# Linear attention with a feed-forward layer: maxima over partitions by GpSimd from batch 2 on, and subtractions in even steps

## The chip, the cores and the metric

The kernel runs on one core of a Trainium2 chip. The metric is the device time of one execution in microseconds (us), lower being better. Engines: PE is TensorE, DVE is VectorE, ACT is ScalarE, POOL is GpSimd, SP is SyncE.

## The reference

Two operators follow each other. The attention has 8 batches of 8 heads, 576 tokens and 64 dimensions, in float32; the feed-forward layer takes its 4608 tokens of 512 values through 2048 hidden values.

```python
q_s = softmax(q, over the head dimension)       # exp(q - max), divided by its sum
k_s = softmax(k, over the 576 tokens)           # exp(k - max), divided by its sum
kv  = einsum('bhsd,bhse->bhde', k_s, v)
x   = einsum('bhsd,bhde->bhse', q_s, kv)        # -> (4608, 512)
h   = x @ w_in                                  # 512 -> 2048
g   = h * erf(softplus(h))
out = g @ w_out                                 # 2048 -> 512
```

The tokens of a batch lie on the partitions, so k's maximum over tokens is one over partitions: 512 maxima (8 heads of 64), each over 576 tokens.

## The kernel before

The feed-forward layer is cut into 48 items. Item n is 384 tokens (`bk`, three blocks to a pair of batches) by 512 hidden values (`g`). Its first product `mm1` is a scheme with seven half-size products in four steps, m n.0 to m n.3. Each product goes into one of three PSUM banks, pX, pY and pZ, of which there is a single copy, and a VectorE add or copy or a ScalarE copy reads it into H: pY by a VectorE copy (line 1010), pX by an add (1012, "X0's add"), pZ and pX by ScalarE copies (1015, 1017), pX by an add (1020, "X2's add"), pZ by an add (1023, "Z's add"), pX by a ScalarE copy (1025). The next product into the same bank waits for its reader. In the text X0, X1, X2, X3 are the four products into pX of one item, in order. Then come T (softplus) and G (erf) on ScalarE, U (`gmul`, line 1078, g = G times H) on VectorE, a cast of g to float16 (1092), `glo` (1096, what the cast left) on VectorE, and, two items later, the second product `mm2` into banks o_0, o_1 and o_2 (line 1124), written out by line 1140 (ob). Items 0 to 5 use float32 products (1037, 1115).

The attention of batches 1 to 7 is one Python generator, `attention(b)`, stepped between the items' parts. Each `yield` gives a share of work (`SHARES`), and a pacer steps the generator until the sum of shares has reached a goal that grows with the item. For items 0 to 5 a string, `ORDER`, says by hand when steps ("A") come; `Z` in it is `wscales`, the scales of the weights from their row sums, with eight transposes through PE. What a step issues goes to in-order engine queues. Where it stands among the other instructions of an engine is set when the program is built, by a scheduler that takes the issued order as priority, unless `tc.issue_after` holds it behind a given instruction.

In a batch: `k_max` takes the maxima over a partition's tokens into `asc[:, 0]` (lines 518, 519, 522). `k_max_T` transposes them on PE (kT, line 529, four pieces) and reduces them on VectorE to km (533). `k_max_rows` spreads km over all partitions by four more transposes (kB, 544). Then k (two halves) and the tail kt are reduced by kB (704, 709), q by its own maxima (`q_sub`, lines 465 and 466, a reduction and a subtraction for each half, and for the pair's tail qt in odd batches), and five or six exponentials follow on ScalarE (349). kv's products are line 565. `all_max` (125, 127) does the same for one column: the scale of x is found from mx, the largest value of kv in a partition, by a transpose into x_bk and a reduction. Lines 301 and 393 split x into a float16 and a rest.

Of the kernel before, what the change touches and what calls it, by code (L numbers as in the profile page):

```python
# [1 line left out]

# [11 lines left out]
ALU = mybir.AluOpType  # L14
AX = mybir.AxisListType
PSUM = bass.MemoryType.PSUM


JOBS = [
# [16 lines left out]
    m0.0 m0.1 D0.0.1 D0.1.1 D1.0 D1.1 m0.2 m0.3 T0 G0 Q0  # L36
    D2.0 A m1.0 D2.1 m1.1 U0 m1.2 m1.3 T1 G1 Q1 A A D3.0 M0.0 D3.1 M0.1 M0.2 Q2 U1 A A
    m2.0 D4.0 m2.1 D4.1 m2.2 m2.3 T2 G2 Q3 A A D5.0 M1.0 D5.1 M1.1 M1.2 U2 A A Q4 D6.0
    m3.0 D6.1 m3.1 D7.0 m3.2 D7.1 m3.3 T3 G3 A A A A A A A A A A Q5 U3 Q6 Q7
    M2.0 M2.1 M2.2 m4.0 m4.1 Z m4.2 m4.3 T4 G4 M3.0 f0 M3.1 M3.2 S0 R0 m5.0 m5.1 U4 m5.2 m5.3  # L40
    T5 G5 f1 S1 R1
"""

# [13 lines left out]
def attn_moe_kernel(  # L57
# [9 lines left out]
    nc = tc.nc  # L67
# [51 lines left out]
    WIN = 7 * 512  # L119


    def all_max(mx, name):

        bk = psa.tile([P, 512], F32, tag="bk", name=f"{name}_bk")
        nc.tensor.transpose(bk[:, :P], mx.to_broadcast([P, P]), ident)
        e = at.tile([P, 1], F32, tag="sc_e", name=f"{name}_e")
        nc.vector.tensor_reduce(e, bk[:, :P], axis=AX.X, op=ALU.max)
        nc.vector.tensor_scalar_max(e, e, TINY)
        return e

    def scale_of_max(mx, name):

        e = all_max(mx, name)
        nc.vector.tensor_scalar(
            e.bitcast(I32), e.bitcast(I32), EXPMASK, None, op0=ALU.bitwise_and
        )
        s = at.tile([P, 1], F32, tag="sx", bufs=3, name=f"{name}_s")
        u = at.tile([P, 1], F32, tag="ux", bufs=3, name=f"{name}_u")
        nc.vector.reciprocal(s, e)
# [330 lines left out]
    def q_norm(t, g, name, b, o=None):  # L470
# [12 lines left out]
        for f in range(2):  # L483
# [86 lines left out]

    E32, QDMA = 2, 3
    kv32 = [t.rearrange("p h c e -> p (h c e)").bitcast(F32) for t in kvh]
    kv32 = [t.rearrange("p (c e) -> p c e", c=NC4) for t in kv32]

# [23 lines left out]
    def kv_split(b, mx):  # L600

        d = bat[b]
        s, u = scale_of_max(mx, f"x{b}")
        d["sx"], d["ux"] = s, u
        if b >= E32:
            hi, lo = (kvh[b % 2][:, i] for i in range(2))
            nc.vector.tensor_scalar_mul(hi, d["kvf"], s)
            nc.vector.scalar_tensor_tensor(
                lo, d["kvf"], s, hi, op0=ALU.mult, op1=ALU.subtract
            )  # L610
        d["U"] = at.tile([P, NG], F32, tag="U", bufs=3, name=f"U_{b}")
        if b > 1:
            nc.vector.tensor_scalar_mul(d["U"], w_u["in"], d["ux"])
# [78 lines left out]
    def attention(b):  # L692
        d, j, p = bat[b], b % 2, b // 2
        even = bat[b - j]
        tl = slice(j * TAIL, (j + 1) * TAIL)
        ks, qs, kt = d["k"], d["q"], even["kt"][tl]
        kmax = k_max(b, ks, (kt, tl))
        yield SHARES[0]
        km = k_max_T(b, kmax)
        q_sub(rows(qs[0]), 16, f"q_{b}_0")  # L700
        yield SHARES[1]
        kb = k_max_rows(b, km)
        for hf in range(2):
            nc.vector.tensor_tensor(
                ks[hf], ks[hf],
                kb[:, None, hf * 4:hf * 4 + 4, :].to_broadcast([P, TM, 4, D]),
                op=ALU.subtract,
            )
        nc.vector.tensor_tensor(kt, kt, kb[tl], op=ALU.subtract)
        yield SHARES[2]  # L710
        q_sub(rows(qs[1]), 16, f"q_{b}_1")
        if j == 1:
            q_sub(even["qt"], H, f"qt_{p}")
        yield SHARES[3]
        for t in (*ks, kt, qs[0], qs[1], *([even["qt"]] if j == 1 else [])):
            act(t, t, AF.Exp, chain=b > 1)
        yield SHARES[4]
        kv_norm(b, 0, kv_mm(b, 0))
        if b > 1:
            d["v"].append(load_half(v, "v", b, 1))  # L720
        q_norm(rows(qs[0]), 16, f"q_{b}_0", b)
        yield SHARES[5]
        if b >= QDMA:
            q_turn_half(b, 0)
        kv_norm(b, 1, kv_mm(b, 1))
        if b + 1 < B:
# [12 lines left out]
        yield SHARES[8]
        for i in ((3 * p + 1, 3 * p + 2) if j else (3 * p, 3 * p + 1)):  # L740
            while not x_free(i):
                yield 0

        def tails():
            if b < QDMA:
                bk = bank(f"qTt_{p}")
                for c in range(NC4):
                    nc.tensor.transpose(
                        bk[:, c * P:(c + 1) * P], asc[:, 1, c * P:(c + 1) * P], ident
                    )  # L750
                even["qtT"] = q_evac(b, 0, bk)
            yield SHARES[9]
            qT = even["qtT"]
            bks = [bank(f"xt_{p}_{a}") for a in range(2)]
            x = xblock(p * NBK + 1)
            for j_ in range(2):
                for hf in range(2):
                    oc = slice(hf * P + j_ * TAIL, hf * P + (j_ + 1) * TAIL)
                    qs_ = [
                        qT[:, :, (2 * hf + c) * P + j_ * TAIL:(2 * hf + c) * P + (j_ + 1) * TAIL]  # L760
                        for c in range(2)
                    ]
# [12 lines left out]
            yield SHARES[10]  # L775

        if j == 1 and b < QDMA:
            yield from tails()
        for hf in range(2):
            if hf == 1 and j == 1 and b >= QDMA:  # L780
                yield from tails()
            qTs = []
            for c in (2 * hf, 2 * hf + 1):
                qTs.append(q_T(b, c, bank(f"qT_{b}_{c}")) if b < QDMA else d["qT"][c])
                if b < QDMA and c % 2 == 1 and b + 1 < B:
                    load_q(b + 1, hf)
# [187 lines left out]
    def mm1(n, k):  # L974
# [29 lines left out]
        def bank2(b):  # L1004
            return s[b][:, :T].rearrange("p (a t) -> p a t", a=2)

        add = nc.vector.tensor_tensor
        if k == 0:
            prod("Y", 1, 1)
            nc.vector.tensor_copy(C[0, 0], bank2("Y"))  # L1010
            prod("X", 0, 0)
            add(C[0, 0], bank2("X"), C[0, 0], op=ALU.add)  # L1012
        elif k == 1:
# [58 lines left out]
    def gmul(n):  # L1072
        s, g = st[n], seq[n][2]
        if n < NG:
            nc.vector.tensor_tensor(flat(s["G"]), flat(s["G"]), flat(s["H"]), op=ALU.mult)
            return
        assert "all" in wready
        nc.vector.scalar_tensor_tensor(  # L1078
            flat(s["G"]), flat(s["G"]), GA32 if n < N32 else GA[:, g:g + 1], flat(s["H"]),
            op0=ALU.mult, op1=ALU.mult,  # L1080
        )
# [11 lines left out]

    def glo(n):
        s = st[n]
        nc.vector.tensor_tensor(flat(s["gl"]), flat(s["G"]), flat(s["gh"]), op=ALU.subtract)  # L1096

    acc = {}

# [177 lines left out]
```

## Time and profile before

| | us |
|---|---|
| median of 3 runs (lowest to highest) | 837.88 (837.61 to 839.1) |
| the profiled execution | 839.42 |
| its span, first to last instruction | 837.6 |
| PE busy | 811.6 (97%) |
| VectorE busy | 624.0 (74%) |
| ScalarE busy | 503.9 (60%) |
| GpSimd busy | 15.9 (2%) |

The profiled execution is one execution, 1.54 us above the median; 1.8 us of it lie outside its span. Busy time of an engine says how long it worked, not whether something waited for it. In the groups of instructions the last column is the engine's idle time just before that group, with what ended it. In the timelines each row has its start, its duration, engine, line, operation, the tiles written and read and the number of merged instructions; brackets hold idle time ahead of it.

### The profile page before, as it was taken

Reading aid. Unit: us, or ns where it says so; the run is one execution under the profiler, and the core shown is the slowest. Engines: PE = TensorE matmul, PEld = TensorE weight load, DVE = VectorE, ACT = ScalarE, POOL = GpSimd, SP = SyncE. Lnnn points to the kernel's source line nnn. Section 1 sums busy time; section 2 is a strip of 40 time slices with the busy share of each in tenths; the row PEclk is TensorE's granted clock in tenths of the full one; section 3 lists DMA queues with packets and bytes.
Section 4 is the critical chain, followed back from the end, with each engine's and each line's share of the span. In section 5 each row is a group of like instructions: output and inputs, shape, how many; then the busy total and the mean of one; then the engine's idle time right before and its main releaser. Section 6 shows DMA issues by size and latency. Waiting matters only on the chain.

```text
span 837.6 us, 15532 instructions
## 1 busy us (share of the span) xinstructions
PE 811.6 (97%) x6546; PEld 547.3 (65%) x6546; DVE 624.0 (74%) x887; ACT 503.9 (60%) x645; POOL 15.9 (2%) x37
## 2 busy tenths in 40 slices
PE   5999999999999999999999999999999999999996
PEld 4555455676666667767676676766776766767762
DVE  6999889998898779767875779857875657554543
ACT  2797759876665746645754556555764565544432
POOL 2101000000000000000000000000000000000000
PEclk9999999999999999999999999999999999999999
DMA  9995710041127205311362204411130100100100
GB/s 259 408 223 183 185 44 38 1 108 39 51 55 154 77 1 105 91 27 27 84 125 51 64 2 93 104 26 27 54 62 14 39 1 1 39 1 1 39 1 38
DMA packets 141348, 61.55 MB, mean 73 GB/s; under 512 B 130528, under 2 KB 132576, under 8 KB 141280
## 3 DMA queue, kind: packets, MB, share of 16 engines
q1 hardware_dynamic: 139104, 52.18, 25.1%
q0 software_dynamic: 2176, 8.39, 2.8%
q8 instruction: 51, 0.84, 0.4%
q14 instruction: 17, 0.14, 0.1%
HBM read 45.09 MB, written 9.44 MB: 65 GB/s over the span
## 4 chain that ended last, share of the span: by engine, by line
PE 59%; DVE 19%; ACT 13%; DMA 4%; issue 3%; SPq 2%; ACTq 0%; DVEq 0%
PE o L1124 25%; PE pX L998 14%; PE pZ L998 6%; ACT G L349 4%; ACT L349 4%; PE pY L998 3%; DVE G L1078 3%; DVE H L1096 2%; PE o L1115 2%; SPq L420 2%; DMA q<-in_q_dram 2%; PE pX L1037 2%; PE kv L565 1%; DVE x L301 1%; PE x L680 1%
## 5 line engine op out<-in xcount | busy, mean ns | idle before, releaser
L1124 PE MATMUL o<-wt,H 128*128 128x512 f16 x1512 | 347.3, 379 | 1.7 <-DVE H L1092 1.3
L998 PEld LDWEIGHTS <-wt 128*128 128x128 f16 x3528 | 293.1, 98 | 37.3 <-issue 15.8
L1124 PEld LDWEIGHTS <-H 128*128 128x128 f16 x1512 | 145.9, 98 | 150.9 <-DVE H L1092 1.8
L998 PE MATMUL pX<-x,wt 128*128 128x192 f16 x2016 | 194.3, 246 | 6.2 <-DVE H L1020 3.3
L349 ACT ACT_TABLE_LOAD x104 | 133.4, 1283 | 8.7 <-DVE H L1023 6.9
L1078 DVE SCALAR_TENSOR_TENSOR G<-G,small,H 128x1536 f32<-128x1536 f32 x44 | 80.0, 1818 | 55.3 <-ACT G L349 55.2
L1025 ACT COPY H<-pX 128x384 f32<-128x384 f32 x42 | 19.9, 474 | 139.2 <-PE pX L998 139.2
L998 PE MATMUL pZ<-x,wt 128*128 128x192 f16 x1008 | 98.4, 246 | 0.0
L349 ACT ACTIVATE G<-H,U 128x768 f32<-128x768 f32 (+1 forms) x56 | 69.2, 1253 | 22.1 <-DVE H L1023 21.5
L1096 DVE TENSOR_TENSOR H<-G,H 128x1536 f16<-128x1536 f32 x42 | 73.7, 1755 | 0.8
L349 ACT ACTIVATE G<-G 128x1536 f32<-128x1536 f32 x48 | 71.2, 1484 | 0.5
L998 PE MATMUL pY<-x,wt 128*128 128x192 f16 x504 | 48.4, 246 | 0.0
L454 ACT ACTIVATE x<-x 128x384 f32<-128x384 f32 (+1 forms) x52 | 16.2, 397 | 48.0 <-PE x L680 48.0
L1023 DVE TENSOR_TENSOR H<-pZ,H 128x384 f32<-128x384 f32 x42 | 23.2, 552 | 26.3 <-PE pZ L998 26.2
L1010 DVE COPY H<-pY 128x384 f32<-128x384 f32 x42 | 23.2, 553 | 26.1 <-PE pY L998 26.0
L300 ACT ACTIVATE x<-x 128x768 f16<-128x768 f32 (+1 forms) x44 | 33.0, 764 | 15.4 <-DVE x L393 15.4
L1092 DVE CAST H<-G 128x1536 f16<-128x1536 f32 x42 | 40.2, 957 | 0.8
L301 DVE SCALAR_TENSOR_TENSOR x<-x,x 128x768 f16<-128x768 f32 (+1 forms) x44 | 37.3, 851 | 3.2 <-ACT x L300 3.2
L1140 DVE TENSOR_SCALAR ob<-o,V 128x512 f32<-128x512 f32 x29 | 21.7, 747 | 21.1 <-PE o L1124 21.1
L1037 PE MATMUL pX<-x,wt 128*128 128x384 f32 x96 | 34.0, 488 | 0.0
L1012 DVE TENSOR_TENSOR H<-pX,H 128x384 f32<-128x384 f32 x42 | 23.3, 555 | 13.7 <-PE pX L998 12.9
L465 DVE TENSOR_REDUCE q_m<-q 128x16 f32<-128x1024 f32 x14 | 17.0, 1216 | 18.0 <-DMA q<-in_q_dram 18.0
(183 smaller groups left out, 818.8 us busy)
## 6 DMA issues: line engine op xcount, KB each, us to landing
out_dram<-ob SPq DMA_DIRECT2D x32, 256.0 KB, 2.3
vbuf<-in_v_dram SPq DMA_DIRECT2D x56, 128.0 KB, 3.2
q<-in_q_dram SPq DMA_DIRECT2D x56, 128.0 KB, 3.2
k<-in_k_dram SPq DMA_DIRECT2D x56, 128.0 KB, 3.2
wt<-in_moe_w_out_dram POOLq DMA_DIRECT2D x5, 1024.0 KB, 6.5
wt<-in_moe_w_in_dram SPq DMA_DIRECT2D x4, 1024.0 KB, 12.0
wt<-in_moe_w_out_dram SPq DMA_DIRECT2D x2, 1024.0 KB, 15.7
H_raw<-in_k_dram SPq DMA_DIRECT2D x2, 512.0 KB, 4.6
```

The costliest lines, as they stand in the source:

```text
L300: nc.scalar.activation(hi, src, AF.Copy, scale=s)
L301: nc.vector.scalar_tensor_tensor(lo, src, s, hi, op0=ALU.mult, op1=ALU.subtract)
L349: i = nc.scalar.activation(out_, in_, func, **kw)
L998: nc.tensor.matmul(o, w[wl][:, c, a * P:(a + 1) * P], x[:, xl, xi, c, :], start=(new and a == 0 and c == 0 and i == 0), stop=(c == 1 and i ...
L1010: nc.vector.tensor_copy(C[0, 0], bank2("Y"))
L1012: add(C[0, 0], bank2("X"), C[0, 0], op=ALU.add)
L1023: add(C[0, 1], bank2("Z"), C[0, 1], op=ALU.add)
L1037: nc.tensor.matmul(ph[:, :T], w[:, c, a * P:(a + 1) * P], x[:, c, :], start=(c == 0), stop=(c == NC4 - 1),)
L1078: nc.vector.scalar_tensor_tensor(flat(s["G"]), flat(s["G"]), GA32 if n < N32 else GA[:, g:g + 1], flat(s["H"]), op0=ALU.mult, op1=ALU.mult,)
L1092: nc.vector.tensor_copy(flat(s["gh"]), flat(s["G"]))
L1096: nc.vector.tensor_tensor(flat(s["gl"]), flat(s["G"]), flat(s["gh"]), op=ALU.subtract)
L1124: nc.tensor.matmul(o, s[gt][:, a, ts_], w[wl][:, a, :], start=(first_ and a == 0 and i == 0), stop=(last_ and a == FG - 1 and i == 2),)
```

## The change

From batch 2 on (`KPOOL = 2`), k's maximum over partitions and the maximum for x's scale are computed by `nc.gpsimd.partition_all_reduce`, which reads and writes SBUF and leaves the result on all partitions. The PE transposes and the VectorE reduction between them are not issued for those batches. k and kt are then reduced by `asc[:, 1]` in SBUF and not by kB in PSUM.

For those batches, the first four yields (2.51, 0, 0.16 and 0.09) become four of 0.69 each: maxima and the GpSimd reduction; both halves of k; kt and q's first half; q's second half and, in odd batches, qt. Each is held behind the last VectorE instruction issued so far by an item's Y copy, adds, gmul or glo (`own` records it, `behind` holds). In `ORDER` eight A's stand where ten did, and Z comes ahead of m4.0 instead of behind m4.1.

```diff
-    m3.0 D6.1 m3.1 D7.0 m3.2 D7.1 m3.3 T3 G3 A A A A A A A A A A Q5 U3 Q6 Q7
-    M2.0 M2.1 M2.2 m4.0 m4.1 Z m4.2 m4.3 T4 G4 M3.0 f0 M3.1 M3.2 S0 R0 m5.0 m5.1 U4 m5.2 m5.3
+    m3.0 D6.1 m3.1 D7.0 m3.2 D7.1 m3.3 T3 G3 A A A A A A A A Q5 U3 Q6 Q7
+    M2.0 M2.1 M2.2 Z m4.0 m4.1 m4.2 m4.3 T4 G4 M3.0 f0 M3.1 M3.2 S0 R0 m5.0 m5.1 U4 m5.2 m5.3
...
-    def all_max(mx, name):
-        bk = psa.tile([P, 512], F32, tag="bk", name=f"{name}_bk")
-        nc.tensor.transpose(bk[:, :P], mx.to_broadcast([P, P]), ident)
+    def all_max(mx, name, pool):
         e = at.tile([P, 1], F32, tag="sc_e", name=f"{name}_e")
-        nc.vector.tensor_reduce(e, bk[:, :P], axis=AX.X, op=ALU.max)
+        if pool:
+            nc.gpsimd.partition_all_reduce(e, mx, P, RED.max)
+        else:
+            ...
...
+    def own(ins):
+        dve[0] = ins.ins
+        return ins
+
+    def behind():
+        return tc.issue_after(dve[0]) if dve[0] else ExitStack()
...
-    E32, QDMA = 2, 3
+    E32, QDMA, KPOOL = 2, 3, 2
...
-        kmax = k_max(b, ks, (kt, tl))
-        yield SHARES[0]
-        km = k_max_T(b, kmax)
-        q_sub(rows(qs[0]), 16, f"q_{b}_0")
-        yield SHARES[1]
-        kb = k_max_rows(b, km)
-        for hf in range(2):
+        with behind():
+            kmax = k_max(b, ks, (kt, tl))
+        def k_sub(hf, kb):
             nc.vector.tensor_tensor(
                 ks[hf], ks[hf],
                 kb[:, None, hf * 4:hf * 4 + 4, :].to_broadcast([P, TM, 4, D]),
                 op=ALU.subtract,
             )
...
+        if b < KPOOL:
+            ...
+        else:
+            kb = asc[:, 1].rearrange("p (h d) -> p h d", h=H)
+            nc.gpsimd.partition_all_reduce(asc[:, 1], asc[:, 0], P, RED.max)
+            step = sum(SHARES[:4]) / 4
+            yield step
+            with behind():
+                for hf in range(2):
+                    k_sub(hf, kb)
+            yield step
+            with behind():
+                nc.vector.tensor_tensor(kt, kt, kb[tl], op=ALU.subtract)
+                q_subs(0)
+            yield step
+            with behind():
+                q_subs(1)
+            yield step
```

In what follows an order of instructions is shown as built, with the tiles written and read; it holds no times. In the changed kernel's numbering k's subtractions are lines 715 and 750, q's 470 and 471, the adds and the Y copy 1049 and 1053, gmul, cast and glo 1121, 1135 and 1139, the splits 306 and 398, ob 1183.

The first place is batch 3, VectorE, before, from glo on: H_1774 is the item's H, and the add from pX in it is X2's add.

```order
L1096 TENSOR_TENSOR H_1556<-G_1770,H_1556 128x1536
L301 SCALAR_TENSOR_TENSOR x_3_1804<-x_1617,x_3_1804 128x768 x2
L533 TENSOR_REDUCE km_1876<-kT_1871 128x4
L1020 TENSOR_TENSOR H_1774<-pX_1789,H_1774 128x2x192
L704 TENSOR_TENSOR k_0_1289<-k_0_1289,kB_1907 128x1024
L704 TENSOR_TENSOR k_1_1294<-k_1_1294,kB_1907 128x1024
L709 TENSOR_TENSOR kt_630<-kt_630,kB_1907 64x512
```

The subtractions of k stand behind X2's add. The same place in the changed kernel, VectorE, from X0's add on (H_1762 is the item's H):

```order
L1049 TENSOR_TENSOR H_1762<-pX_1777,H_1762 128x2x192
L306 SCALAR_TENSOR_TENSOR x_3_1792<-x_1604,x_3_1792 128x384
L715 TENSOR_TENSOR k_0_1278<-k_0_1278,asc 128x1024
L715 TENSOR_TENSOR k_1_1283<-k_1_1283,asc 128x1024
L750 TENSOR_TENSOR kt_630<-kt_630,asc 64x512
L470 TENSOR_REDUCE q_0_m<-q_0_1496 128x16
L1121 SCALAR_TENSOR_TENSOR G_1758<-G_1758,small,H_1543 128x1536
L471 TENSOR_TENSOR q_0_1496<-q_0_1496,q_0_m 128x1024
L1135 CAST H_1543<-G_1758 128x1536
L398 TENSOR_TENSOR x_1604<-x_1604 128x2x192
L1139 TENSOR_TENSOR H_1543<-G_1758,H_1543 128x1536
```

Nine more rows follow (q's second half, qt, splits of x) and then X2's add: the subtractions of k moved ahead of it, between X0's add and X2's. On PE, o_2's twelve products, pZ's twelve, the next item's pY's twelve, twelve of o_0, the kv products of a half and two of o_1 stand between X2 and X3 there; before it was o_2, kB and pZ.

The second place is batch 5, VectorE, before, from glo on; H_3655 is the item's H and H_3802 the next one's.

```order
L1096 TENSOR_TENSOR H_3489<-G_3650,H_3489 128x1536
L301 SCALAR_TENSOR_TENSOR x_6_4038<-x_3426,x_6_4038 128x768
L533 TENSOR_REDUCE km_3767<-kT_3762 128x4
L1023 TENSOR_TENSOR H_3655<-pZ_3697,H_3655 128x2x192
L1010 COPY H_3802<-pY_3803 128x2x192
L1012 TENSOR_TENSOR H_3802<-pX_3817,H_3802 128x2x192
L1140 TENSOR_SCALAR ob_0_3844<-o_0_3345,V_3181 128x512
L704 TENSOR_TENSOR k_0_3088<-k_0_3088,kB_3847 128x1024
```

Between glo and Z's add (line 1023) stand a split and km. In the changed kernel, VectorE, from glo on:

```order
L1139 TENSOR_TENSOR H_3450<-G_3612,H_3450 128x1536
L750 TENSOR_TENSOR kt_2113<-kt_2113,asc 64x512
L470 TENSOR_REDUCE q_0_m<-q_0_3382 128x16
L470 TENSOR_REDUCE qt_m<-qt_2445 128x8
L471 TENSOR_TENSOR q_0_3382<-q_0_3382,q_0_m 128x1024
L471 TENSOR_TENSOR qt_2445<-qt_2445,qt_m 128x512
L470 TENSOR_REDUCE q_1_m<-q_1_3571 128x16
L1049 TENSOR_TENSOR H_3617<-pZ_3661,H_3617 128x2x192
L471 TENSOR_TENSOR q_1_3571<-q_1_3571,q_1_m 128x1024
L1053 COPY H_3766<-pY_3767 128x2x192
L1183 TENSOR_SCALAR ob_0_3808<-o_0_3306,V_3144 128x512
L1049 TENSOR_TENSOR H_3766<-pX_3781,H_3766 128x2x192
```

The subtraction of kt, both of q's halves and qt's tail moved in ahead of Z's add or of the next item's X0 add; both halves of k were done ahead of gmul here.

On POOL the changed kernel has these rows where batch 2 is done (vtail is the tail of v, its memsets were there before):

```order
L742 ISA
L742 ISA asc<-asc 128x512
L449 MEMSET vtail 64x520
L450 MEMSET vtail 64x8
L128 ISA x_e<-mx_1295 128x1
```

The first ISA row without tiles comes once; the other two reductions repeat for each of batches 2 to 7.

More of the change, by code (lines that the diff above doesn't have):

```diff
@@ L4 @@
 import concourse.tile as tile
+from concourse import bass_isa
 from concourse import mybir
@@ L16 @@
 PSUM = bass.MemoryType.PSUM
+RED = bass_isa.ReduceOp
 JOBS = [
@@ L119, in attn_moe_kernel, with scale_of_max @@
     WIN = 7 * 512
-    def all_max(mx, name):
-        bk = psa.tile([P, 512], F32, tag="bk", name=f"{name}_bk")
-        nc.tensor.transpose(bk[:, :P], mx.to_broadcast([P, P]), ident)
+    def all_max(mx, name, pool):
         e = at.tile([P, 1], F32, tag="sc_e", name=f"{name}_e")
-        nc.vector.tensor_reduce(e, bk[:, :P], axis=AX.X, op=ALU.max)
+        if pool:
+            nc.gpsimd.partition_all_reduce(e, mx, P, RED.max)
+        else:
+            bk = psa.tile([P, 512], F32, tag="bk", name=f"{name}_bk")
+            nc.tensor.transpose(bk[:, :P], mx.to_broadcast([P, P]), ident)
+            nc.vector.tensor_reduce(e, bk[:, :P], axis=AX.X, op=ALU.max)
         nc.vector.tensor_scalar_max(e, e, TINY)
         return e
-    def scale_of_max(mx, name):
-        e = all_max(mx, name)
+    def scale_of_max(mx, name, pool):
+        e = all_max(mx, name, pool)
         nc.vector.tensor_scalar(
@@ L490, in q_norm @@
             )
+    dve = [None]
+    def own(ins):
[3 more added lines that the diff above has]
+        return tc.issue_after(dve[0]) if dve[0] else ExitStack()
     def load_kv(b):
@@ L602, in kv_split @@
         d = bat[b]
-        s, u = scale_of_max(mx, f"x{b}")
+        s, u = scale_of_max(mx, f"x{b}", b >= KPOOL)
         d["sx"], d["ux"] = s, u
@@ L708, in attention, with q_subs @@
             )
[L709 to L714, printed above, removed]
+        def q_subs(i):
+            q_sub(rows(qs[i]), 16, f"q_{b}_{i}")
+            if i == 1 and j == 1:
+                q_sub(even["qt"], H, f"qt_{p}")
+        if b < KPOOL:
+            yield SHARES[0]
+            km = k_max_T(b, kmax)
+            q_subs(0)
+            yield SHARES[1]
+            kb = k_max_rows(b, km)
+            for hf in range(2):
+                k_sub(hf, kb)
+            nc.vector.tensor_tensor(kt, kt, kb[tl], op=ALU.subtract)
+            yield SHARES[2]
+            q_subs(1)
+            yield SHARES[3]
+        else:
[4 more added lines that the diff above has]
+            with behind():
+                for hf in range(2):
+                    k_sub(hf, kb)
+            yield step
+            with behind():
+                nc.vector.tensor_tensor(kt, kt, kb[tl], op=ALU.subtract)
+                q_subs(0)
+            yield step
+            with behind():
+                q_subs(1)
+            yield step
         for t in (*ks, kt, qs[0], qs[1], *([even["qt"]] if j == 1 else [])):
@@ L1005, in bank2, with add @@
             return s[b][:, :T].rearrange("p (a t) -> p a t", a=2)
-        add = nc.vector.tensor_tensor
+        def add(*a, **kw):
+            own(nc.vector.tensor_tensor(*a, **kw))
         if k == 0:
             prod("Y", 1, 1)
-            nc.vector.tensor_copy(C[0, 0], bank2("Y"))
+            own(nc.vector.tensor_copy(C[0, 0], bank2("Y")))
             prod("X", 0, 0)
@@ L1077, in gmul @@
         assert "all" in wready
-        nc.vector.scalar_tensor_tensor(
+        own(nc.vector.scalar_tensor_tensor(
             flat(s["G"]), flat(s["G"]), GA32 if n < N32 else GA[:, g:g + 1], flat(s["H"]),
             op0=ALU.mult, op1=ALU.mult,
-        )
+        ))
         if n < N32:
@@ L1095, in glo @@
         s = st[n]
-        nc.vector.tensor_tensor(flat(s["gl"]), flat(s["G"]), flat(s["gh"]), op=ALU.subtract)
+        own(nc.vector.tensor_tensor(flat(s["gl"]), flat(s["G"]), flat(s["gh"]), op=ALU.subtract))
     acc = {}
```

## The prediction

> **What bounds the kernel now.** I read the page's busy table and slices first: is one engine the limit, and where?
>
> ```profile
> PE 811.6 (97%) x6546; PEld 547.3 (65%) x6546; DVE 624.0 (74%) x887; ACT 503.9 (60%) x645; POOL 15.9 (2%) x37
> PE   5999999999999999999999999999999999999996
> ```
>
> TensorE is busy in all slices but the ends, so PE time taken away is worth its full length, unless a wait appears in its place. VectorE has a quarter free, GpSimd nearly everything. Then the groups of instructions by line and shape, for what the change touches:
>
> ```profile
> L529 PE MATMUL kT<-ident,asc 128*128 128x128 f32 x32 | 5.4, 295 | 9.9 <-DVE asc L522 9.9
> L544 PE MATMUL kB<-ident,km 128*128 128x128 f32 x32 | 5.4, 296 | 1.9 <-DVE km L533 1.9
> L125 PE MATMUL x_bk<-ident,mx 128*128 128x128 f32 x8 | 2.2, 275 | 0.1
> L533 DVE TENSOR_REDUCE km<-kT 128x4 f32<-128x512 f32 x8 | 5.5, 686 | 6.2 <-PE kT L529 6.2
> L127 DVE TENSOR_REDUCE x_e<-x_bk 128x1 f32<-128x128 f32 x8 | 2.3, 288 | 5.5 <-PE x_bk L125 5.5
> L858 POOL TENSOR_TENSOR q<-H_raw_q,q_m 128x512 f32<-128x512 f32 x2 | 2.1, 1047 | 9.6 <-DVE q_m L855 9.6
> L465 DVE TENSOR_REDUCE qt_m<-qt 128x8 f32<-128x512 f32 x4 | 2.7, 676 | 0.0
> ```
>
> Each is eightfold, once a batch (kT and kB four pieces); batches 2 to 7 are six eighths. No row reduces over partitions on GpSimd: its 128x512 length, P below, is the unknown.
>
> Last the timelines of the places where a batch's subtractions stand among an item's operations. VectorE runs in order, and each of TensorE's banks pX, pY, pZ waits until an add has read it. Batch 3, VectorE, then TensorE (start, duration):
>
> ```profile
> 219.68 0.69 DVE L522 TENSOR_TENSOR asc<-asc,kt 64x512 f32<-64x512 f32 x1
> 220.40 0.56 DVE L1012 TENSOR_TENSOR H<-pX,H 128x384 f32<-128x384 f32 x1
> 221.34 0.55 DVE L393 TENSOR_TENSOR x<-x 128x384 f32<-128x384 f32 x1
> 221.80 1.21 DVE L465 TENSOR_REDUCE q_m<-q 128x16 f32<-128x1024 f32 x1
> 223.40 1.22 DVE L466 TENSOR_TENSOR q<-q,q_m 128x1024 f32<-128x1024 f32 x1
> 231.47 0.69 DVE L533 TENSOR_REDUCE km<-kT 128x4 f32<-128x512 f32 x1
> 232.08 0.55 DVE L1020 TENSOR_TENSOR H<-pX,H 128x384 f32<-128x384 f32 x1
> 232.91 2.35 DVE L704 TENSOR_TENSOR k<-k,kB 128x1024 f32<-128x1024 f32 x2 [0.28 <-PE kB L544]
> 235.29 0.69 DVE L709 TENSOR_TENSOR kt<-kt,kB 64x512 f32<-64x512 f32 x1
> ```
>
> ```profile
> 226.74 0.60 PE L529 MATMUL kT<-ident,asc 128*128 128x128 f32 x4
> 227.17 1.15 PE L998 MATMUL pX<-x,wt 128*128 128x192 f16 x12
> 228.16 2.75 PE L1124 MATMUL o<-wt,H 128*128 128x512 f16 x12
> 230.75 0.33 PE L998 MATMUL pZ<-x,wt 128*128 128x192 f16 x2
> 232.22 0.65 PE L544 MATMUL kB<-ident,km 128*128 128x128 f32 x4 [1.13 <-DVE km L533]
> 233.53 1.15 PE L998 MATMUL pX<-x,wt 128*128 128x192 f16 x12
> 248.75 0.69 PE L565 MATMUL kv<-vbuf,k 128*64 128x65 f32 x16
> 250.07 1.16 PE L998 MATMUL pZ<-x,wt 128*128 128x192 f16 x12
> ```
>
> In a stream starts lie closer than durations: four transposes cost 0.43 us of PE (226.74 to 227.17), twelve pX 0.99, an o group 2.59 (228.16 to 230.75), a half's kv 1.32 (248.75 to 250.07, 40 pieces). Before, the k subtraction at 232.91 comes *after* the add that frees pX.
>
> **What is removed.** Per batch eight transposes, 0.86 us, and x_bk's at 0.11: 0.97, times six 5.8 us of PE. VectorE loses km, 6 x 0.69, and 6 x 0.29 of x_e, 5.9 us. The wait of 1.13 at kB goes too.
>
> **What is added.** Six reductions of 128x512 and six of 128x1 on GpSimd, which has nothing else to do then but a memset of vtail a batch. The k subtractions wait for the former, the split of x for the latter. P: not below the plain 128x512 pass, 1.05 us; above, seven halvings of 128 partitions at a pass each, 7.3. I take 2.8, the geometric mean: neither end is a reduction, and the row that is nearest is one pass. The 128x1 one replaces a transpose for which VectorE already waits 0.69 (5.5 us over 8): taken as even, between a gain of 0.7 and a loss of P a batch, which the batch's slack before x's split would mostly hide.
>
> **What is moved.** Here the sum is made. The subtractions now come in even steps behind the item's last VectorE operation, so they stand *between* the adds that free TensorE's banks. Durations are from the rows; starts in a stream lie 0.08 closer.
>
> *Batch 3.* From X0's add (220.40) to X2's add (232.08) VectorE had 11.68 us of work. Between the same adds it now has, beyond that: both k subtractions 2.27, kt 0.61, the other q half 1.13 + 1.14, qt's maximum and subtraction 0.61 each, less km 0.61: +5.8. Also k_0 stands 1.0 behind the end of the maxima (220.37 to 221.34) and waits for the rest of P plus 0.1, 1.9 us at 2.8. X2's add ends at about 240.3, the next pX (X3) starts at 240.4. TensorE's new order puts pY 0.99, o 2.59, kv 1.32 and a piece of o 0.43 ahead of it, 5.3 us of useful work. So it stands at 240.4 - 5.3 = 235.1 where it stood at 233.53 before: +1.6, transposes and the kB wait already taken off. With P 1.05 it is -0.1, with 7.3 +6.1.
>
> *Batch 4.*
>
> ```profile
> 287.70 0.56 DVE L1012 TENSOR_TENSOR H<-pX,H 128x384 f32<-128x384 f32 x1
> 291.20 1.22 DVE L465 TENSOR_REDUCE q_m<-q 128x16 f32<-128x1024 f32 x1 [2.94 <-DMA q<-in_q_dram]
> 294.46 1.81 DVE L1078 SCALAR_TENSOR_TENSOR G<-G,small,H 128x1536 f32<-128x1536 f32 x1
> 298.05 1.76 DVE L1096 TENSOR_TENSOR H<-G,H 128x1536 f16<-128x1536 f32 x1
> 299.73 0.55 DVE L1020 TENSOR_TENSOR H<-pX,H 128x384 f32<-128x384 f32 x1
> 300.33 1.15 PE L998 MATMUL pX<-x,wt 128*128 128x192 f16 x12 [2.09 <-DVE H L1020]
> ```
>
> The maximum of q that waits 2.94 for its load is gone from between these adds, a gain: it comes last now. In its place stand the five operations of k's maxima, to about 292.1, gmul, then k_0, which is there by 294 and waits to 295.1 for P. With cast, k_1, glo, a split, kt and q_0's maximum behind it the X2 add ends at about 303.1, against 300.28. TensorE has pY and four o, 1.85, ahead of X3: 303.2 - 1.85 - 300.33 = +1.0, plus 0.5 (estimate) since X0's add itself comes later, behind splits that were moved up, less 0.86 of transposes that stood elsewhere: +0.7 (P 1.05: -0.2; 7.3: +5.2).
>
> *Batches 5 and 7*, one pattern:
>
> ```profile
> 393.55 1.75 DVE L1096 TENSOR_TENSOR H<-G,H 128x1536 f16<-128x1536 f32 x1
> 395.22 0.95 DVE L301 SCALAR_TENSOR_TENSOR x<-x,x 128x768 f16<-128x768 f32 x1
> 401.13 1.15 PE L998 MATMUL pZ<-x,wt 128*128 128x192 f16 x12
> 402.12 1.15 PE L998 MATMUL pX<-x,wt 128*128 128x192 f16 x12
> ```
>
> P is hidden: about 4 us lie between maxima and k_0. But behind glo (to 395.22) now come kt 0.61, q_0's and q_1's maxima and q_0's subtraction 3 x 1.13, qt's two 1.2: Z's add starts at 400.4. Then q_1's subtraction 1.14, a copy 0.47, an ob 0.7, X0's add 0.47: done by 403.75, so the pX of 402.12 starts at 403.85 with 0.43 of o ahead of it: +1.3 each (7.3: +5). The exponentials, later too, now stand on ACT ahead of a copy that frees a pX; I count nothing for it, and it can only add.
>
> *Batches 2 and 6.*
>
> ```profile
> 150.60 1.82 DVE L1078 SCALAR_TENSOR_TENSOR G<-G,small,H 128x1536 f32<-128x1536 f32 x1
> 159.83 2.35 DVE L704 TENSOR_TENSOR k<-k,kB 128x1024 f32<-128x1024 f32 x2 [1.02 <-PE kB L544]
> 167.95 1.15 PE L998 MATMUL pX<-x,wt 128*128 128x192 f16 x12 [0.42 <-ACT H L1025]
> ```
>
> In batch 2 k's and q's maxima now follow gmul and end by my count at 157.1; k_0 follows at 157.1 + 2.8 + 0.2 = 160.1, 0.3 later than before, and so the exponentials and the ACT copy behind them, for which pX waits. Against 0.86 less PE work: -0.6 (P 1.05: -1.2; 7.3: +3.9). Batch 6 has room: -0.7 (7.3: +1). The weights' scales, moved with no operation added, count nothing, within the 0.86 of their eight transposes either way.
>
> **Sum:** -0.6 + 1.6 + 0.7 + 1.3 - 0.7 + 1.3 = +3.6 us, with P 1.05 +0.4, with P 7.3 +26. On the profiled execution's 839.42 that is 843.0; it lies 1.54 above the median of the runs, 837.88, on which it is 841.5. Smaller than 0.2%, 1.7 us, counts as no change.
>
> [...]
>
> **Rivals.** *TensorE's time comes back whole.* The 5.8 us, the 1.13 at kB and about 1 of the 2.09 in batch 4 are gained and the adds are not late enough to stall: -8, 829.9, in part about -4. For it: VectorE idles a quarter of the span, and a late add only hurts when TensorE has nothing else in its order. Against it: in three batches 5 us of VectorE work were put ahead of an add with at most 5.3 of cover. It decides when X2's add of batch 3 ends before 237.
>
> *The gain and the stalls cancel.* P near 1.05: +0.4, 838.3.
>
> *The reduction is long.* Above 5 us k_0 blocks VectorE, in order, with cast, glo and the X adds queued behind, in batches 2 to 5: +13 to +26, 851 to 864. [...]
>
> **How the numbers follow.** Slower by 2 to 12 us, my forecast: 0.42, own range 839.6 to 850. TensorE's time gained, wholly or in part: 0.34. Cancelled: 0.14. Long reduction: 0.10, of which 62 us 0.02. So faster 0.34, same 0.14, slower 0.52. The range leaves out the lowest part of the gain and most of the long case: 831 to 855.
>
> **What would show it.** Right: PE's rows of kT, kB and x_bk fall by six eighths; TensorE's busy time by 5 to 6 us while its idle time grows by 9; waits "<-DVE H" ahead of pX in batches 3, 4, 5 and 7 of 1 to 3 us; GpSimd rows near 2.8 us, with VectorE waiting for them in batches 2 to 4 alone. Wrong: reductions under 1.5 us or over 5, or pX starting without a wait behind the moved subtractions.

## The result: 0.5% slower, and the profile after

| kernel | median us (lowest to highest) | ratio to before (95% interval) |
|---|---|---|
| before | 839.47 (837.61 to 843.57), 13 runs | 1 |
| changed | 843.95 (842.69 to 847.0), 13 runs | 1.0051 (1.0036 to 1.0067) |

The changed kernel takes 4.5 us more by the medians. The prediction had +3.6 us as its sum, 841.5 on the median of three runs that it started from (837.88). The profiled execution of the changed kernel has a span of 842.7 us, 5.1 more than that of before.

The page first, the busy table and TensorE's 40 slices:

```profile
PE 808.1 (96%) x6492; PEld 541.8 (64%) x6492; DVE 621.7 (74%) x875; ACT 503.1 (60%) x645; POOL 30.4 (4%) x49
PE   4999999998989999999999999999999999999997
```

There are 54 TensorE instructions fewer, and TensorE works 3.5 us less. The span is nevertheless longer, and two slices fall from 9 to 8, at 190 to 211 and at 232 to 253 us. So TensorE waits more than it saved: its idle time in the span grew by 8.6 us, from 26.0 to 34.6. The groups by line tell what is left of the transposes, and what a reduction takes (idle time before, and what ended it, in the last column):

```profile
L543 PE MATMUL kT<-ident,asc 128*128 128x128 f32 x8 | 1.8, 360 | 10.9 <-POOL ident masks.py:199 10.6 <-DVE asc L536 0.3
L558 PE MATMUL kB<-ident,km 128*128 128x128 f32 x8 | 1.8, 360 | 0.8 <-DVE km L547 0.8
L742 POOL PARTITION_ALL_REDUCE asc<-asc x6 | 11.2, 1875 | 268.2 <-DVE asc L536 187.8 <-PE pX L1039 80.4
L128 POOL PARTITION_ALL_REDUCE x_e<-mx x6 | 3.0, 497 | 64.5 <-DVE mx L608 64.5
```

kT and kB are down from 32 instructions each to the 8 of batches 0 and 1. A 128x512 reduction took 1.88 us in the mean (1.79 to 1.81 in five of the six, 2.29 in batch 6), one of a single column 0.36 (1.20 the first time). The waits of TensorE for the adds on VectorE, before and after (us in total, times, longest):

```profile
PE pX L998 <- DVE H L1020: 3.3, 3, 2.1
```

```profile
PE pX L1039 <- DVE H L1049: 8.7, 7, 2.3
```

Three waits of 3.3 us became seven of 8.7. (Line 1049 is the add of every bank; in the kernel before no other add than X2's has a wait in this view.) In the places of the prediction, batch 3, VectorE and then TensorE:

```profile
222.39 0.56 DVE L1049 TENSOR_TENSOR H<-pX,H 128x384 f32<-128x384 f32 x1
222.86 1.14 DVE L306 SCALAR_TENSOR_TENSOR x<-x,x 128x384 f16<-128x384 f32 x1
224.38 2.36 DVE L715 TENSOR_TENSOR k<-k,asc 128x1024 f32<-128x1024 f32 x2 [0.37 <-POOL asc L742]
240.51 0.68 DVE L471 TENSOR_TENSOR qt<-qt,qt_m 128x512 f32<-128x512 f32 x1
241.11 0.55 DVE L1049 TENSOR_TENSOR H<-pX,H 128x384 f32<-128x384 f32 x1
```

```profile
238.82 0.61 PE L1167 MATMUL o<-wt,H 128*128 128x512 f16 x2
241.72 1.93 PE L1039 MATMUL pX<-x,wt 128*128 128x192 f16 x12 [2.29 <-DVE H L1049]
243.44 0.85 PE L1039 MATMUL pZ<-x,wt 128*128 128x192 f16 x4
```

From X0's add to X2's add it is 18.7 us now (222.39 to 241.11), where it was 11.7; TensorE runs out of work and waits 2.29. The twelve products behind that wait take 1.72 us where twelve take 0.99 elsewhere; more on that at the end. Batch 4, GpSimd, VectorE and TensorE:

```profile
294.99 1.79 POOL L742 PARTITION_ALL_REDUCE asc<-asc  x1 [34.08 <-PE pX L1039]
295.38 2.25 DVE L1121 SCALAR_TENSOR_TENSOR G<-G,small,H 128x1536 f32<-128x1536 f32 x1 [0.56 <-ACT G L354]
297.56 1.21 DVE L715 TENSOR_TENSOR k<-k,asc 128x1024 f32<-128x1024 f32 x1
304.97 0.54 DVE L1049 TENSOR_TENSOR H<-pX,H 128x384 f32<-128x384 f32 x1
305.56 1.15 PE L1039 MATMUL pX<-x,wt 128*128 128x192 f16 x12 [1.58 <-DVE H L1049]
```

Batch 5, VectorE and TensorE:

```profile
402.79 0.55 DVE L1049 TENSOR_TENSOR H<-pZ,H 128x384 f32<-128x384 f32 x1
405.51 0.55 DVE L1049 TENSOR_TENSOR H<-pX,H 128x384 f32<-128x384 f32 x1
403.39 1.15 PE L1039 MATMUL pZ<-x,wt 128*128 128x192 f16 x12 [0.18 <-DVE H L1049]
406.11 1.15 PE L1039 MATMUL pX<-x,wt 128*128 128x192 f16 x12 [1.14 <-DVE H L1049]
```

And one place that the prediction did not have, GpSimd at the start, before and after:

```profile
1.68 0.29 POOL masks.py:199 TENSOR_SCALAR_AFFINE_SELECT ident<-ident 128x128 f32<-128x128 f32 x1
```

```profile
10.24 0.28 POOL masks.py:199 TENSOR_SCALAR_AFFINE_SELECT ident<-ident 128x128 f32<-128x128 f32 x1 [8.65 <-DMA H_raw_q<-in_q_dram]
```

The select that makes the identity matrix comes 8.6 us later, and the first transposes, which need it, start at 10.57 instead of 8.65.

How the difference grows is read from the starts of each item's first pY product in both traces, changed minus before:

| up to | us in before | us behind | change in this stretch |
|---|---|---|---|
| the last float32 items before batch 2's maxima | 85 | 1.44 | start +1.4 |
| item 10 | 218 | 1.99 | batch 2 +0.6 |
| item 13 | 268 | 4.31 | batch 3 +2.3 |
| item 18 | 350 | 2.80 | batch 4 -1.5 |
| item 25 | 461 | 4.45 | batch 5 +1.7 |
| item 30 | 541 | 4.09 | batch 6 -0.4 |
| item 36 | 635 | 5.51 | batch 7 +1.4 |
| end of the span | 837.6 | 5.15 | -0.4 |

### The profile page after: what moved, and what is told of

Read it like the earlier page. It is cut to its first block, busy times and chain, and to the rows that moved or that the text cites. A ratio compares the mean times of both kernels' runs of the same rounds, so it can differ in the third digit from the quotient of the medians.

```text
span 842.7 us, 15440 instructions
## 1 busy us (share of the span) xinstructions
PE 808.1 (96%) x6492; PEld 541.8 (64%) x6492; DVE 621.7 (74%) x875; ACT 503.1 (60%) x645; POOL 30.4 (4%) x49
## 4 chain that ended last, share of the span: by engine, by line
PE 53%; DVE 11%; ACT 6%; issue 3%; ACTq 0%; DVEq 0%
PE o L1167 26%; PE pX L1039 14%; PE pZ L1039 7%; PE pY L1039 3%; ACT L354 2%; ACT G L354 2%; DVE G L1121 2%; PE kv L579 1%; DVE x L306 1%; DVE q_m L470 1%; DVE k L715 1%; DVE H L1139 1%; DVE x L398 1%; PE x L694 1%; DVE H L1049 1%
## 5 line engine op out<-in xcount | busy, mean ns | idle before, releaser
L1049 DVE TENSOR_TENSOR H<-pX,H 128x384 f32<-128x384 f32 x84 | 46.4, 553 | 20.6 <-PE pX L1039 19.8
L459 ACT ACTIVATE x<-x 128x384 f32<-128x384 f32 (+1 forms) x52 | 16.2, 397 | 51.8 <-PE x L694 51.8
L1080 PEld LDWEIGHTS pX<-x,wt 128*128 128x128 f32 x96 | 17.8, 190 | 13.6 <-issue 1.4
```

The source lines that it names most:

```text
L1049: own(nc.vector.tensor_tensor(*a, **kw))
L1080: nc.tensor.matmul(ph[:, :T], w[:, c, a * P:(a + 1) * P], x[:, c, :], start=(c == 0), stop=(c == NC4 - 1),)
```

## The experiments

All ratios are to the kernel before, run on the same chip beside the experiment.

**One reduction, in a kernel that is otherwise that of before.**

```diff
...
         d["sx"], d["ux"] = s, u
+        if b == 7:
+            junk = at.tile([P, 1], F32, tag="junk", bufs=1, name="junk")
+            nc.gpsimd.partition_all_reduce(junk, mx, P, bass_isa.ReduceOp.max)
```

> The kernel before, with one 128x1 reduction over partitions on GpSimd added in batch 7, whose result nobody reads. Theory (start): a program that holds such a reduction pays at its start, where the first select on GpSimd that makes the identity came at 10.24 us instead of 1.68; the first transposes then start at 10.5 instead of 8.65 and the time grows by 1 to 2 us, with all else as before. Rival (late adds alone): the start of the changed kernel was an accident of one profile; the time is that of the kernel before within 0.2%, and the select comes at 1.7 us.

Measured: 840.15 us against 837.62 of before beside it, ratio 1.0029 (1.0006 to 1.0051). GpSimd's timeline:

```profile
10.28 0.28 POOL masks.py:199 TENSOR_SCALAR_AFFINE_SELECT ident<-ident 128x128 f32<-128x128 f32 x1 [8.71 <-DMA H_raw_q<-in_q_dram]
```

The select is as late as in the changed kernel, though the reduction itself comes at the end of the program. So the late start is no accident. In the profile the products lie 1.75 us behind at 27 us and 1.36 at 268; by 301 us all but 0.24 of it is made up in waits that the kernel before has there. So in this one execution little of the start's cost was left at the end; the times say 0.5 to 4.3 us.

**The reductions alone,** in the places of before, nothing held.

```diff
-            step = sum(SHARES[:4]) / 4
-            yield step
-            with behind():
-                for hf in range(2):
-                    k_sub(hf, kb)
...
+            yield SHARES[0]
+            q_subs(0)
+            yield SHARES[1]
+            for hf in range(2):
+                k_sub(hf, kb)
+            nc.vector.tensor_tensor(kt, kt, kb[tl], op=ALU.subtract)
+            yield SHARES[2]
+            q_subs(1)
+            yield SHARES[3]
```

> GpSimd's reductions from batch 2 on, but the yields, the places and the hand-written order as in the kernel before, and nothing held behind the items' operations. Theory (late adds): the loss comes from the subtractions' places; without them TensorE's 5.8 us come back less 1 to 2 us at the start and about 1 us where k waits for the reduction: 3 us faster than before, 2 to 5. Rival (the reductions themselves, by VectorE waiting for GpSimd): no faster than the changed kernel, +4 us against before.

Measured: 854.37 us, ratio 1.0176 (1.0139 to 1.0213), 15 us slower: against my theory, and worse than its rival. The waits of VectorE on the reduction, and of TensorE on the adds and on ACT's copies:

```profile
DVE k L714 <- POOL asc L741: 7.2, 5, 2.0
```

```profile
PE pX L1034 <- DVE H L1044: 11.8, 12, 3.1
PE pX L1034 <- ACT H L1055: 5.5, 6, 2.5
```

The scheduler put k_0 right behind the maxima (in batch 5 with one ob between them); VectorE then stands for up to 2.0 us, five times, with gmul, cast, glo and the adds behind it. That it did so because no transposes and no bank of PSUM stand between maxima and subtraction any more is argued, not shown.

**The steps alone,** maxima by transposes.

```diff
...
-            nc.gpsimd.partition_all_reduce(asc[:, 1], asc[:, 0], P, RED.max)
+            km = k_max_T(b, kmax)
             step = sum(SHARES[:4]) / 4
             yield step
+            kb = k_max_rows(b, km)
```

> The four even steps held behind the items' operations and the changed hand-written order, but all maxima by TensorE's transposes as before, none on GpSimd. Theory (late adds): VectorE's subtractions stand ahead of the adds as in the changed kernel; no 1 to 2 us at the start, no gain of 5.8 us on TensorE: slower than before by 6 to 11 us, slower than the changed kernel. Rival (the reductions themselves): the time of the kernel before, within 2 us.

Measured: 846.77 us, ratio 1.0101 (1.0066 to 1.0135). The time is as the theory had it: the steps cost some 9 us where TensorE keeps its transposes. The trace does not put all of that on late adds:

```profile
PE pX L1039 <- DVE H L1049: 4.5, 5, 1.3
PE kT L543 <- DVE asc L536: 11.1, 5, 8.7
```

The waits for the adds are 1.2 us more than before, because the wait of 2.1 in batch 4 is gone while new ones of 1.1 to 1.3 stand in batches 3, 5 and 7. The transposes, which now wait for held maxima, have 1.2 more, and kv's products 1.3 for exponentials that come later. (This profiled execution took 850.82 us, 4 above the median, with a wait of 2.3 at 109 us that is in no other trace.) In batch 3 X2's add costs TensorE a wait of 1.13 here and of 2.29 in the changed kernel, so there the reduction adds to the steps. The reductions, put into these steps, are worth 4 us by the ratios (1.0051 against 1.0101, with intervals that just touch), less than the 5.8 us of TensorE's time.

**The identity on VectorE** in the changed kernel.

```diff
-    make_identity(nc, ident)
...
+    nc.vector.memset(ident, 0.0)
+    nc.vector.memset(seq_[:, :1], 0.0)
+    for w in (1, 2, 4, 8, 16):
+        nc.vector.tensor_scalar_add(seq_[:, w:2 * w], seq_[:, :w], float(w))
+    nc.vector.transpose(seqT, seq_)
+    for i in range(4):
+        s_ = slice(32 * i, 32 * i + 32)
+        nc.vector.tensor_scalar(ident[s_, s_], seq_[s_], seqT[s_, :1], None, op0=ALU.is_equal)
```

> The changed kernel, with the identity made on VectorE (counting along the free axis, a 32x32 transpose, comparisons) in place of GpSimd's select. Theory (start): the first transposes are back at about 8.7 us and 1 to 2 us of the loss go, 842.5 where the changed kernel has 844. Rival: the start is hidden behind loads later on, the time is that of the changed kernel within 0.3 us.

Measured: 841.81 us, ratio 1.0039 (1.002 to 1.0058), 1 us less than the changed kernel's 1.0051, with intervals that overlap. What TensorE's first transposes wait for is VectorE's maxima again:

```profile
PE kT L552 <- DVE asc L545: 11.3, 2, 8.5
```

That the start is mended is shown: at 36 us the products lie 0.23 us behind the kernel before, and 1.70 in the changed kernel. What that is worth in the time is not settled. The profiled execution, of 845.32 us, 3.5 above the median, loses 4.9 us again at 66 us, where transposes wait 2.8 for batch 1's maxima and the products behind them run slowly (the granted clock is 0.52 from 65 to 70 us).

**The reduction twice.**

```diff
             nc.gpsimd.partition_all_reduce(asc[:, 1], asc[:, 0], P, RED.max)
+            nc.gpsimd.partition_all_reduce(asc[:, 1], asc[:, 1], P, RED.max)
```

> The changed kernel, with a second reduction of the same 128x512 tile behind the first (its result is the same), so that k waits for 3.6 us where it waited for 1.8. Theory (even steps leave about 2 us free behind the maxima, in batches 2 to 4 no more): batch 2 loses 1.0, batch 3 1.8, batch 4 1.0, batches 5 to 7 nothing: 3 to 4 us slower than the changed kernel, ratio to before about 1.009. Rival (the wait is hidden by other work of VectorE): within 0.5 us of the changed kernel, 1.005.

Measured: 849.82 us, ratio 1.0138 (1.0118 to 1.0158), 7 us more than the changed kernel, twice what I expected.

```profile
DVE k L715 <- POOL asc L743: 4.5, 3, 1.7
```

```profile
PE pX L1040 <- DVE H L1050: 11.8, 7, 3.0
```

VectorE waits for it in three places, for 4.5 us in all where it was 0.6 in two. That is the 3 to 4 us of the theory; the rest is in batch 6 (a wait of 2.1 where it was 1.4) and in products that run slowly behind a long wait (the mean granted clock of this execution is 0.996, that of the changed kernel's 0.998). So the even steps hide about 2 us in batches 2 to 4 and no more.

**Nothing held behind the items' operations.**

```diff
-        return tc.issue_after(dve[0]) if dve[0] else ExitStack()
+        return ExitStack()
```

> The changed kernel with its four even steps, but nothing held behind the items' operations, so that the scheduler may place the steps' instructions where its priorities put them. Theory (the even steps give the reduction time, the hold only fixes the place): within 2 us of the changed kernel. Rival (the hold is what keeps k's subtraction from standing directly behind the maxima, and so VectorE from waiting for the reduction): slower by 6 to 10 us, like the reductions alone, ratio to before 1.012 to 1.018, with VectorE waits on the reduction of over 5 us in all.

Measured: 852.64 us, ratio 1.0155 (1.0133 to 1.0176). The rival is right: the hold, not the even shares, keeps k off the reduction.

```profile
DVE k L715 <- POOL asc L742: 6.6, 5, 2.0
```

**The hand-written order as before.**

```diff
-    M2.0 M2.1 M2.2 Z m4.0 m4.1 m4.2 m4.3 ...
+    M2.0 M2.1 M2.2 m4.0 m4.1 Z m4.2 m4.3 ...
```

(and ten A's for eight.) 

> The changed kernel, with the hand-written order as before: ten A's and the weights' scales behind m4.1. Theory (counted at nothing, within 0.9 us): within 1 us of the changed kernel, ratio to before 1.004 to 1.006. Rival (batch 2's place matters): 2 us or more apart from it, either way, with the difference between 100 and 165 us in the trace.

Measured: 842.54 us, ratio 1.005 (1.0031 to 1.007): the changed kernel's 1.0051. Counting it at nothing fits, within the 1.6 us that the interval leaves either way.

**Wider steps**, with the identity on VectorE.

```diff
-            step = sum(SHARES[:4]) / 4
+            step = 0.8
...
-                q_subs(1)
+                q_sub(rows(qs[1]), 16, f"q_{b}_1")
+            yield step
+            with behind():
+                q_sub(even["qt"], H, f"qt_{p}") if j == 1 else None
...
-        yield SHARES[4]
+        yield SHARES[4] - (0.5 if b >= KPOOL else 0)
```

(and 0.74 less at the next yield.) 

> The changed kernel, with the identity made on VectorE, five steps in place of four (maxima; both halves of k; kt and q's first half; q's second half; qt) and 0.8 of share each where it was 0.69, taken from the two yields behind. So less of VectorE's work stands between two adds: at most 13 us between X0's add and X2's in batch 3 where it was 17.5, and 4 us ahead of a Z add where it was 7 to 8. Theory (late adds): the stalls of 2.3 and 1.6 us in batches 3 and 4 and of 1.1 in 5 and 7 fall to under 0.5 each, and the start's 1 to 2 us go: 5 to 7 us faster than the changed kernel, 1 to 2 us faster than before. Rival (TensorE's 5.8 us are lost for another reason): within 2 us of the changed kernel with the identity on VectorE, 1.004 times before.

Measured: 842.38 us, ratio 1.0042 (1.0026 to 1.0057): a miss, no better than the identity alone (1.0039). Less work ahead of each add did not take the waits away, it moved them: between 220 and 700 us TensorE's waits of over a microsecond are then at 236 us (2.7), 305 (1.6), 323 (1.3), 406 (1.1), 496 (1.6), 514 (1.6) and 598 (1.1).

**Only k's subtractions held**, three shares behind the maxima, and the same **with q's between**. Both have the identity on VectorE; the diff is that of the first.

```diff
-        with behind():
-            kmax = k_max(b, ks, (kt, tl))
+        kmax = k_max(b, ks, (kt, tl))
...
+            yield .69
+            q_subs(0)
+            yield .69
+            q_subs(1)
+            yield .69
             with behind():
                 for hf in range(2):
                     k_sub(hf, kb)
-            yield step
-            with behind():
                 nc.vector.tensor_tensor(kt, kt, kb[tl], op=ALU.subtract)
...
+            yield .69
```

> GpSimd's reductions with the identity made on VectorE; the maxima of k and the subtractions of q are not held and may go early, and only the subtractions of k and kt are held, three shares of 0.69 behind the maxima. In the order as built 11 to 34 us of VectorE's work then stand between maxima and subtraction of k. Theory (both losses are places: k directly behind its reduction when nothing is held, too much VectorE work ahead of an add when all is held): TensorE's 5.8 us come back, no wait of VectorE on a 128x512 reduction, TensorE's waits for adds as before: 4 to 6 us faster than before, ratio 0.993 to 0.995. Rival (the reduction itself disturbs VectorE wherever it stands, or the maxima in floating block a new place): not faster than before, ratio 1.000 or more.

> As in the run with only k's subtractions held, but these come sooner: the first half one share of 0.69 behind the maxima, the second with q's first half, kt with q's second; 16 to 24 us of VectorE's work between maxima and k in batches 4 to 7, 1 in batch 3. Theory: 4 to 5 us faster than before, about 1 us behind the other for batch 3. Rival: as there, 1.000 or more.

Measured: 851.44 us, ratio 1.0141 (1.0115 to 1.0167), and 843.75, ratio 1.0051 (1.0037 to 1.0065). Both miss. In the second TensorE waits 10.0 us for the adds, as in the run with wider steps. In the first no VectorE wait on a 128x512 reduction is left; a part of TensorE's waits changed engine:

```profile
PE pX L1044 <- ACT H L1065: 9.4, 5, 2.3
PE pX L1044 <- DVE H L1054: 6.5, 6, 2.5
```

Batch 5 shows it, ACT and then TensorE:

```profile
409.47 2.00 ACT L363 ACTIVATE k<-k 128x1024 f32<-128x1024 f32 x2
414.05 0.61 ACT L363 ACTIVATE qt<-qt 128x512 f32<-128x512 f32 x1
414.92 0.48 ACT L1065 COPY H<-pX 128x384 f32<-128x384 f32 x1
```

```profile
415.45 1.76 PE L1044 MATMUL pX<-x,wt 128*128 128x192 f16 x10 [2.31 <-ACT H L1065]
```

k's exponentials come so late that ACT has all six directly ahead of the copies that free pZ and pX. So hiding the reduction is not enough; k's subtraction has a latest place too.

**Batches 2 and 6 alone, and batches 3, 4, 5 and 7 alone**, with the identity on VectorE, the second also with the hand-written order of before.

```diff
-    E32, QDMA, KPOOL = 2, 3, 2
+    E32, QDMA, KPOOL = 2, 3, (2, 6)
...
-        if b < KPOOL:
+        if b not in KPOOL:
```

> GpSimd's reductions and the even, held steps in batches 2 and 6 alone, where the prediction's sum has a gain (-0.6 and -0.7 us); all other batches by TensorE's transposes and in the places of before; the identity made on VectorE, so that the start costs nothing. Theory (the sum's terms add up batch by batch): 1.3 us faster than before, ratio 0.998, 0.997 to 1.000. Rival (a reduction costs something wherever it stands, or the start is not mended by the identity): 1.001 to 1.004.

> The complement: GpSimd's reductions and the even, held steps in batches 3, 4, 5 and 7, batches 2 and 6 and the hand-written order as before, the identity on VectorE. Theory: the sum's terms +1.6, +0.7, +1.3 and +1.3 are 4.9 us slower than before, 1.65 more where TensorE's clock halves behind the wait in batch 3; ratio 1.005 to 1.008, and together with the run of batches 2 and 6 the changed kernel with the identity on VectorE (1.004). Rival (the batches are not independent): outside of 1.003 to 1.009, or waits ahead of pX in other batches than 3, 4, 5 and 7.

Measured: 840.0 us, ratio 1.0023 (1.001 to 1.0037), a miss, and 842.45, ratio 1.0049 (1.0034 to 1.0065), at the lower edge of what was expected. The first shows that batch 6 is no gain. TensorE there:

```profile
494.14 1.15 PE L1048 MATMUL pX<-x,wt 128*128 128x192 f16 x12 [1.53 <-DVE H L1058]
```

Batch 6 has batch 4's pattern, with both halves of k, kt and q_0's maximum between gmul and X2's add; in the kernel of the other batches, where batch 6 is as before, that wait is not there. The two ratios together give 1.0072, against 1.0039 for all six batches; with these intervals I can't say whether the batches are independent.

None of the twelve kernels, nor the changed one, is faster than the one before, and no run points to one that would be.

## Why the prediction was right, and where its steps were off

*The way it goes.* Right, and the waits for late adds are the largest part of it, but not enough by themselves. In the views of TensorE's waits the sum went from 20.9 to 30.0 us, 9.1 more; the span is then accounted for: 9.1 of waits and 1.65 of slow products, less 5.8 of transposes, are 4.95, and the span grew by 5.15. Of the 9.1 the adds have 5.8 (3.3 to 9.1, pX and pZ together), just what the transposes gave back; 1.5 are transposes of q that wait for ACT, 1.0 the transposes kT, whose first wait is 1.9 longer. The prediction's waits ahead of pX in batches 3, 4, 5 and 7 are there, with 2.29, 1.58, 1.14 and 1.14 us. But it had 9 us of idle time, most of it behind adds, and TensorE's busy time 5 to 6 us down; it fell by 3.5. So what made the kernel slower, and not merely the same, is in good part what the sum left out, and that the sum came within 1 us of the 4.5 is partly luck. The rival that TensorE's time comes back whole had its deciding point before 237 us, at X2's add in batch 3: that add came at 241.11.

*The length of the reduction.* Taken as 2.8, measured 1.88: between one pass and my geometric mean. By the prediction's own slopes in batches 2 to 4 that is nearly 2 us less. VectorE's wait for it was 0.25 us in batch 2, in batch 3 0.37 and not 1.9, and batch 4 had none.

*A cost left out.* The start: +1.4 us by 85 us, in the changed kernel and in the one with a single reduction. The change's description of GpSimd's part stopped at what each reduction takes; that in a program with such a reduction another operation on GpSimd comes later, by 8.6 us here, was in no step. These two errors about cancel, which is luck.

*Batch by batch*, predicted and measured: batch 2 -0.6 and +0.6, batch 3 +1.6 and +2.3, batch 4 +0.7 and -1.5, batch 5 +1.3 and +1.7, batch 6 -0.7 and -0.4, batch 7 +1.3 and +1.4. The prediction adds these up as if each batch's delay lasted to the end. It does not: delay that a batch brings along is swallowed where the kernel before waits anyway. In the run with one reduction, where batch 4 is untouched, 1.36 us of delay at 268 us are 0.24 at 301; in the run of batches 3, 4, 5 and 7, where batch 6 is untouched, batch 6's stretch gives back 0.6. So a measured figure is not that batch's own price.

Batches 5 and 7 are as worked out row by row: Z's add comes 2.4 us later than the 400.4 of the prediction, when the products were 2.4 to 2.8 late. Batch 3 contains 1.65 us of slow products; with the identity on VectorE, where they ran at full speed behind the same wait of 2.3, the same stretch cost 1.1. Batch 4 came out 2.2 lower. TensorE's wait of 2.09, behind VectorE's wait for the load of q, went as the prediction had it, and one of 1.58 is left. But k_0, which was to wait for a reduction of 2.8, found it done (296.78, k_0 at 297.56), and the 0.5 for a later X0's add rested on no row; how much of the rest is batch 3's delay swallowed there stays open. Batch 2's 0.6 is in its last part, where a transpose of q waits 0.9 us more for ACT (1.77 at 209 us, 0.86 before), which I did not follow that far. Batch 6, "has room", was taken from the order and not worked out: its wait is 1.4 us, and since its stretch gives back 0.6 where batch 6 is untouched, the 0.4 here is no gain of its own.

*The reduction beside VectorE's operations.* The sum counted nothing for it. The row of batch 4 shows gmul beside the reduction (294.99 to 296.78), 2.25 long instead of 1.81: 0.44 us lost. A split of the weights took 1.45 instead of 0.69 beside batch 2's, and was over before it:

```profile
160.54 1.81 POOL L742 PARTITION_ALL_REDUCE asc<-asc  x1 [65.59 <-DVE asc L536]
```

```profile
160.67 1.45 DVE L332 TENSOR_TENSOR wt<-wt 128x512 f32<-128x512 f32 x1
```

So in these two rows an operation of VectorE took 0.4 to 0.8 us longer beside a reduction, and did not wait for its end (gmul was done at 297.63, 0.85 behind it), as far as the profile's spans on GpSimd can tell. No run shows the 62 us that have 0.02 of the chances: the six reductions of 128x512 in the changed kernel took 1.79 to 2.29.

## What to carry to other kernels

Taking work from a saturated engine is worth its length only if nothing that it waits for gets later: list, for each buffer that the engine waits for, what now stands ahead of its reader, and how much other work the engine has in its order to cover it. An operation with a latency on another engine needs a place for its consumer that is neither directly behind it (7 us of waits here) nor so late that the next engine's burst blocks another buffer (9 us). Before adding up what each place costs, ask where the program waits anyway: a delay that reaches such a wait is swallowed there (1.36 us became 0.24 in the run with one reduction). And look at the start of the program when it uses a new kind of GpSimd instruction anywhere: here the first select came 8.6 us later.

## What the runs showed of the hardware that I had not expected

*GpSimd's first select.* In the six programs with a reduction over partitions and this select, the select ran at 10.24 to 11.49 us instead of 1.68; with the steps alone, without a reduction, it ran at 1.68. The profile names a load as its releaser, 8.65 us in the changed kernel, but the kernel of before has the same loads and no such wait, and in the reductions alone it names none. What the 8.6 us are made of no run shows.

*TensorE slowed down behind a long wait.* Behind the 2.29 us wait of batch 3 the products ran at half their pace until 245.3, 1.65 us lost; the granted clock is 0.58 from 241.7 to 243 us and 0.50 from 243 to 245. The rows of the stretches have the window, its length, the busy time of PE, PEld, DVE, ACT and POOL, the granted clock, DMA's share and GB/s:

```profile
241.70:243.00 1.30, 1.28 (x10) 1.23 (x10) 1.30 (x4) 0.16 (x1) 0.00 (x0) 0.58 0.66 150
243.00:245.00 2.00, 2.00 (x15) 1.90 (x13) 1.64 (x4) 1.30 (x2) 0.00 (x0) 0.50 0.86 195
```

The fourteen traces of this case have 24 gaps of 2 us and more between float16 products (start to start, less the usual interval). Behind 13 of them such a stretch follows, with 1.3 to 2.8 us lost each; behind the others, that of batch 4 in the kernel before among them, none does, nor behind any gap under 2 us. So in these traces a wait of over 2 us could cost most of its length again (1.65 us behind 2.29), and a sum of waits alone is too low.

Which gaps are followed can be read from the traces. The records of the granted clock change only at whole multiples of 3.41 us after the first one, in all fourteen. Cut into windows on that grid, up to 10 us before the end, 18 windows at full clock were followed by half clock (the 13, and five with a gap beside float32 products), and in all of them TensorE was busy for at most 42.7% by the profile; in the other 3309 it was busy for at least 44.9%, and none was followed. In the traces of the changed kernel and of the kernel before alone it was 33.0% in the one that was followed, and at least 51.8% in the other 474. The rows are batch 3 in the changed kernel (busy 1.13 of 3.42 us, then half clock) and batch 4 in the kernel before (1.76 of 3.41, then full clock):

```profile
238.49:241.91 3.42, 1.13 (x19) 0.67 (x16) 3.42 (x6) 1.74 (x3) 0.00 (x0) 1.00 0.37 83
241.91:245.32 3.41, 3.41 (x24) 3.24 (x22) 2.73 (x7) 1.62 (x2) 0.00 (x0) 0.50 0.82 186
```

```profile
296.47:299.88 3.41, 1.76 (x16) 1.26 (x15) 3.38 (x4) 0.00 (x0) 0.00 (x0) 1.00 0.00 0
299.88:303.29 3.41, 2.96 (x36) 2.96 (x36) 1.42 (x3) 1.76 (x2) 0.00 (x0) 1.00 0.00 0
```

So in these traces a gap of 2 to 3 us was followed by half clock when most of it fell into one window, and was not when an edge of the grid divided it, as the edge at 299.88 us does in the second pair of rows. The same wait of 2.3 in batch 3 cost 1.65 us in the changed kernel's execution, and nothing in that with the identity on VectorE, where the twelve products behind it took 0.99.
